# Two row pairs of a 2x2 block product taken by halves in turn, and y kept in empty thirds of its blocks until it is stored

## The chip, the core and the metric

The kernel runs on one core of a Trainium2 chip. The core has TensorE (PE; its weight loads are listed apart as PEld), VectorE (DVE), ScalarE (ACT), GpSimd (POOL) and SyncE (SP), each with its own instruction queue, and 16 DMA engines that all queues share. The metric is device microseconds of one execution. Before the change it is 2008.89 us, the median of three runs (2005.96 to 2012.94).

## The reference

First a long causal convolution along the sequence, written with FFTs; then a mixing layer whose large part is two products with 5696 x 5696 matrices:

```python
batch, seq, d_model = (8, 5696, 128)
# convolution: x (8, 5696, 128), h (5696, 128)
Yf = np.fft.rfft(x, n=2*S, axis=1) * np.fft.rfft(h, n=2*S, axis=0)[None]
x = np.fft.irfft(Yf, n=2*S, axis=1)[:, :S, :]
# mixing
theta = x @ w_theta
zr, zi = x * np.cos(theta), x * np.sin(theta)
y = np.einsum('ts,bsd->btd', w_tok_r, zr) + np.einsum('ts,bsd->btd', w_tok_i, zi)
u = x + y
out = u + np.maximum(u @ w_ch, 0.0)
```

Inputs and output are float32.

## The kernel before

**Set-up and convolution.** Tables of sines and cosines are made first: `r_index` and `r_table` for `r_u`, `r_v`, and `e_index` and `e_table` for `e_t`, in nine steps `E_STEPS` of four columns. For a table GpSimd writes an index and rounds it, VectorE subtracts (`below_one`, L164) and takes the absolute value (`absolute`, L167), and ScalarE takes the sines. While the set-up is written, `tc.manual_schedule` keeps VectorE, ScalarE and GpSimd in the order of the code; a second such block, for VectorE and ScalarE, begins after `load_x(1)`, with `below_one(*r_at[n])` as its first lines. An instruction that stands in no such block, or in another one, is placed by the framework's scheduler. Then eight groups of the convolution follow, each with stages A (`a`), spectrum (`f`), products (`p`, `q`, L400), C (`c`) and D (`d`), in the order of the strings `PLAN_X`, `PLAN_0` and `PLAN`; `t` in `PLAN_0` is a step of `e_table`. The convolved x, called y in the code, goes to `yt_hbm`, channels first.

**Phase steps.** For each of the 22 tiles of 128 tokens of the first half of the sequence, and for each half `hh` of the batch, `phase_step` transposes y into PSUM (`tpz`, L759), computes theta on TensorE (L545 to L551), copies y to SBUF (`copy`, L764), stores it in `y2_hbm` (L765; the profile writes `y_hbm`), takes sine and cosine on ScalarE (L556 to L558), and multiplies on VectorE (L569, L570) to zr and zi. The SBUF place of y is one of six in turn, in the tail of block 0 (`ring["all"]`). The steps of the first batch half (`steps0`) run beside the last convolution group; those of the second (`steps1`) run inside the first row pair, one after every second product, in the order `order1`.

**Blocks.** z is cut into 11 blocks of 128 contraction rows (`b`, `j` = 0 to 10) for the first half of the sequence (pass `p` = 0), and 11 for the second (`p` = 1). A block tile has seven parts of 1024 elements: the first four are the raw zr and zi of both batch halves, the other three take sums of these (`sum_ops`, L852), which only the seven-product scheme reads; two more sums are made in place over raw parts. The second batch half of blocks 0 to 8 is written straight into the block (`home_of`, L583, queues of SP and POOL), and their first half is loaded from `zr_hbm` by `load_b_half` (L741, POOL's queue). Blocks 9 and 10 go through `zr_hbm` whole and are loaded after the last step by `load_b` (L727, ACT's queue).

**Row pairs.** Weight rows `tt` and `22 + tt` make a pair; with `w_tok_r` and `w_tok_i` as columns that is a 2x2 block product. Pairs 0 and 1 of pass 0 use the plain eight products (`plain`, L1247), all others a seven-product scheme (L1326), with sums of weights made by VectorE. Contraction runs in stretches of three blocks (`TJ`), two stretches to a chunk of weights, the second of the second chunk with two blocks. Weights come in by GpSimd's queue (`load_w`, L650, four DMAs for each of a chunk's four operands) into a ring of six places; VectorE transposes them (`w_t`, L919), one stretch ahead (`prepare`), into five and four buffers. `chunks` sets the order: all stretches of pair 0, then all of pair 1, and so on. The loop over `stretches` writes the program; `i` is the stretch's number. At `i == 1` the first two stretches of pair 0 are multiplied with the 22 steps between the products, then come `i == 2` (by batch halves) and the rest. VectorE follows the order of the code up to block 6 of pair 2.

**Around it.** `sum_some` puts owed block sums between products. At a pair's end its PSUM banks are added to y (`addend` loads it from `y2_hbm` or `yt_hbm`) and the result goes to `cp_hbm` (`finish`). `aside` writes a background step (`spread`: phases of the second half of the sequence, `bg_phase`, and small weight transposes, `bg_left`) into stretches that do not end a pair.

Of the kernel before, what the change touches and what calls it, by code (L numbers as in the profile page):

```python
# [10 lines left out]
F32 = mybir.dt.float32  # L11
# [12 lines left out]
def kernel(  # L24
# [683 lines left out]

    place_of, home_of = {}, {}

# [35 lines left out]
    def phase_step(ti, hh, store=nc.sync, odd_eng=None):  # L746

        st = sides["phases"]
        yT = st["end"][ti] if hh == 0 and ti in st["end"] else st[hh][:, :, ti * P:(ti + 1) * P]
        if hh:  # L750
            tags_ = ((f"m{M2}", f"m{M6}"), (f"m{M4}", "misc"))[len(steps1) % 2]
            theta_ps = mps.tile([P, 512], F32, tag=tags_[0], name="theta_ps")
            tpz = mps.tile([P, 4, P], BF16, tag=tags_[1], name="tpz")
        else:
            ps = psum()
            theta_ps = ps[:, 0, :]
            tpz = ps[:, 1, :].bitcast(BF16)[:, :512].rearrange("p (b t) -> p b t", b=4)
        for b in range(4):
            nc.tensor.transpose(tpz[:, b, :], yT[:, b, :], ident_bf)  # L759
        k = st["n"] = (st.get("n", 0) + 1) % 6  # L760
        y_ap = ring["all"][:, WB + 4096 + 512 * k:WB + 4608 + 512 * k].rearrange("p (b d) -> p b d", b=4)

        def copy():
            nc.vector.tensor_copy(y_ap, tpz)  # L764
            store.dma_start(y2_hbm[ti].rearrange("p b d -> p (b d)")[:, 512 * hh:512 * hh + 512],  # L765
                          y_ap.rearrange("p b d -> p (b d)"))
# [89 lines left out]

    done = {"used": 0}
    owed = []

    def sum_some(n):  # L860
# [278 lines left out]

    nxt, second, st = None, None, {}  # L1140
    ordered = ExitStack()
    for i, (k, p, tt, j0, s0, nj) in enumerate(stretches):
        if (p, tt, j0 + s0) in ((0, 0, 0), (1, 0, 0)):
            ordered.enter_context(tc.manual_schedule(engines={mybir.EngineType.DVE}))
        elif (p, tt, j0 + s0) in ((0, 2, 6), (1, 1, 0)):
            ordered.close()
        first_of_pair = j0 + s0 == 0
        end_of_pair = j0 + s0 + nj == NJ
        if first_of_pair and tt == pairs[p][0]:
            if p == 1:  # L1150
                start_pass(p)
            else:
                nxt = prepare(0)
                ms = [mps.tile([P, 512], F32, tag=f"m{q}", name=f"m{q}") for q in (M3, M5, M1, M7)]
                pool_order.enter_context(tc.manual_schedule(engines={mybir.EngineType.Pool}))
# [76 lines left out]
        if first_of_pair and i:  # L1232
            ms = [mps.tile([P, 512], F32, tag=f"m{q}", name=f"m{q}") for q in (range(7) if not classic else (M3, M4, M5, M2) if p else (M2, M6, M1, M7))]
        if first_of_pair:
            where = ((tt, 1), (22 + tt, 0), (tt, 0), (22 + tt, 1))
            if zl is not None:
# [7 lines left out]
        def product(a, jj, j, n, hs):  # L1244
            for r in range(2):
                for h in hs:
                    nc.tensor.matmul(ms[n // 2 * 2 + h], a[n][:, j, :, r],  # L1247
                                     bts_of[p][jj][n % 2 * 2 + h][:, r, :],
                                     start=(n % 2 == 0 and jj == 0 and r == 0), stop=False)

        if i == 0:
            continue
        if i == 1:
            for q, (h, s) in enumerate(((0, 0), (0, 1), (1, 0), (1, 1))):
# [13 lines left out]
        if i == 2:  # L1268
            for h in range(2):
                for n in range(4):  # L1270
                    for j in range(nj):
                        product(a, j0 + s0 + j, j, n, (h,))
                        if j != 1 and h + n:
                            sum_some(1)
            continue
        if classic:
            for n in range(4):
                for j in range(nj):
                    product(a, j0 + s0 + j, j, n, range(2))
# [27 lines left out]
        else:  # L1307
# [4 lines left out]
            if end_of_pair:  # L1312
# [4 lines left out]
                        M1: ((c11, c11, add), (c22, c22, add)),  # L1317
                        M7: ((c11, c11, add),), M6: ((c22, c22, add),)}
            while owed and owed[0][0] < j0 + s0 + nj:
                sum_some(1)  # L1320
            for n, q in enumerate(ORDER):
# [67 lines left out]
```

## Time and profile before

| | us |
|---|---|
| median of three runs | 2008.89 |
| the profiled execution's own time | 2009.51 |
| its span in the trace | 2007.7 |
| convolution with the first batch half's steps | 0 to 363 |
| second batch half's steps, in pair 0 | 363 to 418 |
| rest of pair 0 | 418 to 447 |
| pair 1 | 447 to 486 |
| pairs from 2 on, both passes | 486 to 2007.7 |

All times in the views are microseconds from the span's start, unless marked ns. In a timeline row stand start, duration, engine, line, operation, output<-inputs, shapes and count; the bracket at the end is the engine's idle time before it and what ended that. A row of waits has who waited and for what, then total, times and longest. A window row has, for each engine, busy time and number of instructions, then TensorE's granted clock as a share of full speed, the share of the DMA engines' time that was busy, and what they moved. A row of DMA issues has the queue (SPq, ACTq, POOLq), the count, the size of one and the median time from issue to landing. Buffer numbers are left out of names.

### The profile page before, as it was taken

Reading aid. Unit: us, or ns where it says so; the run is one execution under the profiler, and the core shown is the slowest. Engines: PE = TensorE matmul, PEld = TensorE weight load, DVE = VectorE, ACT = ScalarE, POOL = GpSimd, SP = SyncE. Lnnn points to the kernel's source line nnn. Section 1 sums busy time; section 2 is a strip of 40 time slices with the busy share of each in tenths; the row PEclk is TensorE's granted clock in tenths of the full one; section 3 lists DMA queues with packets and bytes.
Section 4 is the critical chain, followed back from the end, with each engine's and each line's share of the span. In section 5 each row is a group of like instructions: output and inputs, shape, how many; then the busy total and the mean of one; then the engine's idle time right before and its main releaser. Section 6 shows DMA issues by size and latency. Waiting matters only on the chain.

```text
span 2007.7 us, 41091 instructions
## 1 busy us (share of the span) xinstructions
PE 1920.4 (96%) x15581; PEld 1064.4 (53%) x15757; DVE 1557.9 (78%) x2897; ACT 646.5 (32%) x965; POOL 963.0 (48%) x1727
## 2 busy tenths in 40 slices
PE   5898998789999999999999999999999999999998
PEld 5798997544444444444444444444444444444444
DVE  7977887776888888888876779677686776867767
ACT  5998997832323233332300001011111111111112
POOL 7633223463445454453656555545545455354550
PEclk8999999989999999999999999999999999999999
DMA  9989779997899999898999799878869778787893
GB/s 123 60 96 144 91 111 231 279 226 137 151 180 176 181 162 170 173 184 167 178 169 146 136 267 215 134 135 143 151 123 157 135 138 151 130 148 142 141 156 82
DMA packets 489238, 312.02 MB, mean 155 GB/s; under 512 B 184471, under 2 KB 450199, under 8 KB 488055
## 3 DMA queue, kind: packets, MB, share of 16 engines
q0 software_dynamic: 321504, 154.90, 61.6%
q1 hardware_dynamic: 160368, 140.73, 23.9%
q10 hardware_dynamic: 7168, 13.76, 1.9%
q8 instruction: 123, 2.02, 0.4%
q14 instruction: 75, 0.61, 0.1%
HBM read 354.37 MB, written 90.29 MB: 221 GB/s over the span
## 4 chain that ended last, share of the span: by engine, by line
PE 66%; DVE 4%; DMA 3%; issue 2%; ACT 0%; POOL 0%; DVEq 0%
PE m L1326 61%; DVE c L1333 2%; DMA b<-z_hbm 1%; PE utp L999 1%; PE v L1006 1%; PE m L1330 1%; DVE wt L919 1%; PE m L1214 1%; PE theta_ps L534 0%; PE tpz L947 0%; DMA c<-cp_hbm 0%; DMA cp_hbm<-c 0%; DMA z_hbm<-mag 0%; DVE b L852 0%; PE m L1247 0%
## 5 line engine op out<-in xcount | busy, mean ns | idle before, releaser
L650 POOL DMA_DIRECT2D ring<-in_moe_w_tok_i_dram x720 | 388.3, 547 | 652.4 <-DVE wt L919 559.5
L919 DVE STREAM_TRANSPOSE wt<-ring 128x384 f32<-128x384 f32 (+2 forms) x720 | 359.1, 523 | 121.9 <-PE m L1326 57.2
L650 POOL DMA_DIRECT2D ring<-in_moe_w_tok_r_dram x720 | 387.1, 549 | 122.7 <-DVE wt L919 68.8
L1326 PE MATMUL m<-b,wt 128*128 128x512 bf16 x1605 | 384.8, 379 | 4.1 <-DVE wt L919 2.1
L1326 PEld LDWEIGHTS <-wt 128*128 128x128 bf16 x1804 | 176.0, 98 | 216.5 <-DVE wt L919 5.1
L1333 DVE TENSOR_TENSOR c<-c,m 128x512 f32<-128x512 f32 x412 | 265.2, 668 | 0.4 <-PE m L1326 0.4
L1001 ACT ACTIVATE ring<-utp 128x512 bf16<-128x512 bf16 x85 | 50.7, 597 | 575.2 <-PE utp L999 575.2
L139 POOL DMA_DIRECT2D x<-in_x_dram x128 | 99.1, 790 | 119.0 <-PE ps L255 110.5
L421 PE MATMUL ps<-r_u,uv 128*128 128x128 f16 x1024 | 125.6, 222 | 11.0 <-DVE uv L400 6.4
L421 PEld LDWEIGHTS <-uv 128*128 128x128 f16 x2048 | 120.8, 99 | 13.0 <-DVE uv L400 6.7
L421 PE MATMUL ps<-r_v,uv 128*128 128x128 f16 x1024 | 125.2, 221 | 0.0
L1247 PE MATMUL m<-b,wt 128*128 128x512 bf16 x471 | 112.7, 387 | 12.8 <-DMA b<-zr_hbm 9.1
L400 DVE TENSOR_TENSOR uv<-xs,hs 128x1024 f16<-128x1024 f16 x192 | 117.7, 661 | 7.5 <-ACT xs L396 5.9
L996 ACT ACTIVATE ub<-c 128x512 bf16<-128x512 f32 x88 | 55.1, 629 | 185.8 <-DMA ring<-wl_hbm 103.8
L396 ACT ACTIVATE xs<-ps 128x1024 f16<-128x1024 f32 x96 | 88.2, 994 | 4.5 <-PE ps L278 1.6
L1247 PEld LDWEIGHTS <-wt 128*128 128x128 bf16 x528 | 51.5, 99 | 70.5 <-issue 14.9
L949 ACT ACTIVATE ring<-tpz 128x512 bf16<-128x512 bf16 (+1 forms) x46 | 27.4, 597 | 145.9 <-PE tpz L947 127.2
L536 ACT ACTIVATE red<-theta_ps,magic 128x512 f32<-128x512 f32 (+1 forms) x46 | 31.6, 687 | 129.9 <-PE theta_ps L534 101.3
L1008 DVE SCALAR_TENSOR_TENSOR c<-v,c 128x512 f32<-128x512 f32 x88 | 59.8, 682 | 2.6 <-PE v L1006 2.6
L852 DVE TENSOR_TENSOR b<-b 128x1024 bf16<-128x1024 bf16 x100 | 61.3, 680 | 0.0
L278 PEld LDWEIGHTS <-w_t 64*128 64x128 f16 x3240 | 54.2, 97 | 12.1 <-issue 5.9
L556 ACT ACTIVATE mag<-red 128x512 f32<-128x512 f32 (+1 forms) x46 | 29.0, 631 | 92.9 <-DVE red L538 92.9
(2927 smaller groups left out, 3643.2 us busy)
## 6 DMA issues: line engine op xcount, KB each, us to landing
ring<-in_moe_w_tok_r_dram POOLq DMA_DIRECT2D x352, 96.0 KB, 4.6
ring<-in_moe_w_tok_i_dram POOLq DMA_DIRECT2D x352, 96.0 KB, 4.9
ring<-in_moe_w_tok_r_dram POOLq DMA_DIRECT2D x352, 80.0 KB, 4.5
ring<-in_moe_w_tok_i_dram POOLq DMA_DIRECT2D x352, 80.0 KB, 4.0
cp_hbm<-c SPq DMA_DIRECT2D x88, 256.0 KB, 2.3
c<-cp_hbm SPq DMA_DIRECT2D x88, 256.0 KB, 4.4
out_dram<-c SPq DMA_DIRECT2D x88, 256.0 KB, 4.3
yy<-y_hbm SPq DMA_DIRECT2D x84, 128.0 KB, 2.4
```

The costliest lines, as they stand in the source:

```text
L139: nc.gpsimd.dma_start(x16[p0:p1, e, n0:n0 + 16, :HD], bass.AP(tensor=src.tensor, offset=src.offset + (p0 * N2 + n0) * D + dh * HD, ap=[[N2 ...
L396: nc.scalar.activation(xs[:, :, :, :CHK[c][1]], ps, AF.Copy)
L400: nc.vector.tensor_tensor(uv[e][:, :, :, c0:c0 + ck], xs_of[c][:, e:e + 1, :, :ck].to_broadcast([P, 2, HD, ck]), h_part(c), op=mult)
L421: nc.tensor.matmul(o, uv_t[e][:, r, d * K1:d * K1 + P], r_, start=(r == 0), stop=(r == 1))
L650: nc.gpsimd.dma_start(wb[32 * i:32 * i + 32, :ng, :nj * 64], bass.AP(tensor=a.tensor, offset=a.offset + row0 * S + p * H + i * QR + j0 * 6 ...
L852: return [lambda f=f, x=x: f(*x) for f, x in ((nc.vector.tensor_sub, (bt[M3], b12, b22)), (nc.vector.tensor_sub, (bt[M4], b21, b11)), (nc. ...
L919: nc.vector.transpose(wt.rearrange("p j t r -> p (j t r)").bitcast(F32).rearrange("p (j g t) -> p g j t", j=TJ, g=4)[:, :ng, :nj], wb[:, : ...
L996: nc.scalar.activation(ub[:m].rearrange("p b d -> p (b d)"), c[:m], AF.Copy)
L1008: nc.vector.scalar_tensor_tensor(c[:m], v[:m], 0.0, c[:m], op0=ALU.max, op1=ALU.add)
L1247: nc.tensor.matmul(ms[n // 2 * 2 + h], a[n][:, j, :, r], bts_of[p][jj][n % 2 * 2 + h][:, r, :], start=(n % 2 == 0 and jj == 0 and r == 0), ...
L1326: nc.tensor.matmul(ms[q], a[q][:, j, :, r], bts[jj][q][:, r, :], start=(jj == 0 and r == 0), stop=(jj == NJ - 1 and r == 1 and q not in left))
L1333: nc.vector.tensor_tensor(c, z, ms[q], op=op)
```

## The change

It has three parts. In the set-up, `below_one` of both r tables, and the VectorE part of steps 1 and 2 of the e table (`e_turns`), move to the end of the first ordered block, ahead of `load_x(1)`. The first two row pairs are multiplied by halves in turn: blocks 0 to 5 of pair 0, blocks 0 to 5 of pair 1, then 6 to 10 of pair 0, and 6 to 10 of pair 1; so both pairs hold four PSUM banks at once, and no background step runs in pair 1. The y's of the last seven steps of `steps0` and of all of `steps1` are kept in the empty thirds of blocks 4, 3, 7, 8 and 6 (`y_tails`, 512 elements each). Except for tiles 0 and 1 their stores are put off to stretches 2 to 5, where each is written behind a named matmul on SP's queue (`y_some`), and SP now follows the order of the code from pair 0 to block 6 of pair 2. Sums of a block wait until its y's are stored and 28 matmuls have been written since. The first halves of blocks 3 and 4 are loaded inside `steps1` in place of before it.

```diff
-    def e_table(n, n0, cn):
+    def e_turns(n, n0, cn):
         t, k = e_pair(n, cn)
         below_one(t, k)
         absolute(k, t)
+
+    def e_sines(n, n0, cn):
+        t, k = e_pair(n, cn)
         t3, k3 = (z.rearrange("p (n m) -> p n m", m=NB) for z in (t, k))
         sine(e_t[:N1, n0:n0 + cn, 1, :], t3, -1)
         cosine(e_t[:N1, n0:n0 + cn, 0, :], k3)
+
+    def e_table(n, n0, cn):
+        if n not in (1, 2):
+            e_turns(n, n0, cn)
+        e_sines(n, n0, cn)
...
+    for n in range(2):
+        below_one(*r_at[n])
+    for e_ in E_STEPS[1:3]:
+        e_turns(*e_)
     load_x(1)
     e_index(*E_STEPS[4])
     in_order.close()
     in_order.enter_context(tc.manual_schedule(engines={mybir.EngineType.DVE, mybir.EngineType.Activation}))
-    for n in range(2):
-        below_one(*r_at[n])
...
-    chunks = [(p, tt, c) for p in range(2) for tt in pairs[p] for c in range(len(CHUNKS))]
+    chunks = [(0, tt, c) for c in range(len(CHUNKS)) for tt in pairs[0][:2]]
+    chunks += [(p, tt, c) for p in range(2) for tt in pairs[p][2 - 2 * p:] for c in range(len(CHUNKS))]
...
-        k = st["n"] = (st.get("n", 0) + 1) % 6
-        y_ap = ring["all"][:, WB + 4096 + 512 * k:WB + 4608 + 512 * k].rearrange("p (b d) -> p b d", b=4)
+        if y_tails:
+            j, at = y_tails.pop(0)
+            y_flat = place_tail[j][:, at:at + 512]
+        else:
+            j, k = None, (st.get("n", 0) + 1) % 6
+            st["n"] = k
+            y_flat = ring["all"][:, WB + 4096 + 512 * k:WB + 4608 + 512 * k]
...
             nc.vector.tensor_copy(y_ap, tpz)
-            store.dma_start(y2_hbm[ti].rearrange("p b d -> p (b d)")[:, 512 * hh:512 * hh + 512],
-                          y_ap.rearrange("p b d -> p (b d)"))
+            if j is None or ti < 2:
+                y_store()
+            else:
+                y_late.append((j, lambda: y_store(nc.sync)))
...
+    def y_some(n, behind=None):
+        for _ in range(min(n, len(y_late))):
+            j, store = y_late.pop(0)
+            ins = store()
+            y_at[j] = done["n"]
+            if behind is not None:
+                tc.add_manual_dep(ins.ins, behind.ins.name, mybir.DependencyInfo(
+                    mybir.DependencyClass.Sync, mybir.DependencyReason.DATA), reason="y store")
...
-        for o in [o for o in owed if o[1] <= 2 or done["used"] > o[0]][:n]:
+        for o in ([o for o in owed if o[1] <= 2 or done["used"] > o[0]] if forced else
+                  [o for o in owed if (o[1] <= 2 or done["used"] > o[0]) and o[0] < done["ready"] and done["n"] - y_at.get(o[0], -99) > 28
+                   and all(j != o[0] for j, _ in y_late)])[:n]:
             owed.remove(o)
+            while any(j == o[0] for j, _ in y_late):
+                y_some(1)
             o[2]()
+
+    def new_tails(j):
+        place_tail[j] = place_of[j] if j in place_of else home_of[j]
+        y_tails.extend((j, 4096 + 512 * q) for q in range(6))
...
-    for j in range(1, 5):
+    for j in (4, 3):
+        new_tails(j)
+    for j in range(1, 3):
         load_b_half(j)
...
+    for j in (7, 8):
+        place_of[j] = new_b(j, home_pool(j))
+        new_tails(j)
+    new_tails(6)
...
-            if len(steps1) in (17, 18):
+            if len(steps1) in (17, 18, 19, 20):
                 load_b_half(23 - len(steps1))
...
-            ordered.enter_context(tc.manual_schedule(engines={mybir.EngineType.DVE}))
+            ordered.enter_context(tc.manual_schedule(
+                engines={mybir.EngineType.DVE} if p else {mybir.EngineType.DVE, mybir.EngineType.SP}))
...
-            if first_of and spread and (p == 1 or (tt > 0 and (tt, j0 + s0) != (1, 0) and not end_of_pair)):
+            if first_of and spread and (p == 1 or (tt > 1 and not end_of_pair)):
...
-            ms = [mps.tile([P, 512], F32, tag=f"m{q}", name=f"m{q}") for q in (range(7) if not classic else (M3, M4, M5, M2) if p else (M2, M6, M1, M7))]
+            tags_ = ([f"m{q}" for q in (range(7) if not classic else (M3, M4, M5, M2))] if p or not classic
+                     else [f"m{M4}", f"m{M2}", f"m{M6}", "misc"])
+            ms_of[tt] = [mps.tile([P, 512], F32, tag=t_, name=t_) for t_ in tags_]
+        ms = ms_of[tt]
...
                     for j in range(nj):
-                        product(a, j0 + s0 + j, j, n, (h,))
+                        last = product(a, j0 + s0 + j, j, n, (h,))
                         if j != 1 and h + n:
                             sum_some(1)
+                        if j == 1:
+                            y_some(1, last)
+            done["used"] = j0 + s0 + nj
...
                 for j in range(nj):
-                    product(a, j0 + s0 + j, j, n, range(2))
+                    last = product(a, j0 + s0 + j, j, n, range(2))
                     if p == 0 and (n * nj + j) % 4 != 3:
                         sum_some(1)
+                    if p == 0 and (n * nj + j) % 3:
+                        y_some(1, last)
...
-            if p == 0:
-                done["used"] = tt * (j0 + s0 + nj)
+            if p == 0 and tt:
+                done["used"] = j0 + s0 + nj
...
             while owed and owed[0][0] < j0 + s0 + nj:
-                sum_some(1)
+                sum_some(1, True)
```

More of the change, by code (lines that the diff above doesn't have):

```diff
@@ L707 @@
     bts_of = {0: [], 1: []}
-    place_of, home_of = {}, {}
+    place_of, home_of, place_tail = {}, {}, {}
+    y_tails, y_late = [], []
     def new_b(j, pool):
@@ L1138, in in_place @@
             op()
-    nxt, second, st = None, None, {}
+    nxt, second, st, ms_of = None, None, {}, {}
     ordered = ExitStack()
@@ L1153 @@
                 nxt = prepare(0)
-                ms = [mps.tile([P, 512], F32, tag=f"m{q}", name=f"m{q}") for q in (M3, M5, M1, M7)]
+                ms_of[0] = [mps.tile([P, 512], F32, tag=f"m{q}", name=f"m{q}") for q in (M3, M5, M1, M7)]
                 pool_order.enter_context(tc.manual_schedule(engines={mybir.EngineType.Pool}))
@@ L1232 @@
         if first_of_pair and i:
-            ms = [mps.tile([P, 512], F32, tag=f"m{q}", name=f"m{q}") for q in (range(7) if not classic else (M3, M4, M5, M2) if p else (M2, M6, M1, M7))]
+            tags_ = ([f"m{q}" for q in (range(7) if not classic else (M3, M4, M5, M2))] if p or not classic
+                     else [f"m{M4}", f"m{M2}", f"m{M6}", "misc"])
+            ms_of[tt] = [mps.tile([P, 512], F32, tag=t_, name=t_) for t_ in tags_]
+        ms = ms_of[tt]
+        where = ((tt, 1), (22 + tt, 0), (tt, 0), (22 + tt, 1))
         if first_of_pair:
-            where = ((tt, 1), (22 + tt, 0), (tt, 0), (22 + tt, 1))
             if zl is not None:
@@ L1246, in product @@
                 for h in hs:
-                    nc.tensor.matmul(ms[n // 2 * 2 + h], a[n][:, j, :, r],
+                    ins = nc.tensor.matmul(ms[n // 2 * 2 + h], a[n][:, j, :, r],
                                      bts_of[p][jj][n % 2 * 2 + h][:, r, :],
                                      start=(n % 2 == 0 and jj == 0 and r == 0), stop=False)
+            done["n"] += 2 * len(hs)
+            return ins
         if i == 0:
             continue
+        done["ready"] = max(done["ready"], 2 * TJ if tt else j0 + s0 + nj)
         if i == 1:
@@ L1318 @@
                         M7: ((c11, c11, add),), M6: ((c22, c22, add),)}
+            assert not y_late
             while owed and owed[0][0] < j0 + s0 + nj:
-                sum_some(1)
+                sum_some(1, True)
             for n, q in enumerate(ORDER):
```

8 lines of the change are left out of this document (6 added, 2 removed).

## The prediction

> **What bounds the kernel now.** I read the page first, then TensorE's waits, then single stretches. Its lines for the span, the engines and the slices in time:
>
> ```profile
> span 2007.7 us, 41091 instructions
> ...
> PE 1920.4 (96%) x15581; PEld 1064.4 (53%) x15757; DVE 1557.9 (78%) x2897; ACT 646.5 (32%) x965; POOL 963.0 (48%) x1727
> ...
> PE   5898998789999999999999999999999999999998
> ...
> PEclk8999999989999999999999999999999999999999
> ```
>
> TensorE is busy from slice 9 (450 us) to the end. Nothing in the change takes a matmul away, so all there is to win lies ahead of that: the set-up, the 22 phase steps with batches 4 to 7 that run inside the first row pair, and what follows them. Windows by stage (columns: busy of PE, PEld, DVE, ACT, POOL, then granted clock, DMA share, GB/s):
>
> ```profile
> 363.00:418.00 55.00, 47.38 (x394) 29.77 (x401) 43.91 (x83) 41.55 (x71) 32.06 (x60) 0.95 0.98 288
> 418.00:428.50 10.50, 10.45 (x49) 4.79 (x49) 7.44 (x15) 0.00 (x0) 6.33 (x13) 1.00 1.03 204
> 428.50:447.20 18.70, 11.40 (x41) 4.37 (x40) 9.89 (x19) 1.08 (x2) 10.23 (x20) 0.73 1.06 207
> 447.20:486.00 38.80, 38.59 (x195) 18.27 (x196) 27.28 (x48) 9.64 (x16) 12.06 (x23) 1.00 0.68 125
> ```
>
> The third row is the last stretch of the first pair (blocks 9, 10): 11.40 us busy of 18.70 at clock 0.73. The DMA engines are full up to 447 us and have room after it (0.68).
>
> **Part 1, the set-up.** TensorE's and then VectorE's waits between 30 and 62 us (total, times, longest), and from the timeline the operations that are moved:
>
> ```profile
> PE ps L255 <- DVE h L333: 1.9, 2, 1.6
> PE ps L255 <- DVE a__753 L260: 0.6, 1, 0.6
> ...
> DVE uv L400 <- ACT xs L396: 2.6, 1, 2.6
> DVE r_1t L164 <- POOL r_1k L161: 1.8, 1, 1.8
> DVE r_0t L164 <- POOL r_0k L161: 1.1, 1, 1.1
> ```
>
> ```profile
> 37.09 0.29 DVE L164 SCALAR_TENSOR_TENSOR r_0t<-r_0k,r_0t 128x128 f32<-128x128 f32 x1 [1.14 <-POOL r_0k L161]
> ...
> 62.06 0.52 DVE L164 SCALAR_TENSOR_TENSOR e_all<-e_all 89x356 f32<-89x356 f32 x1
> ...
> 62.62 0.34 DVE L167 TENSOR_SCALAR e_all<-e_all 89x356 int32<-89x356 int32 x1
> ```
>
> Although `below_one(r_at)` stands behind the first stage A in the code, VectorE ran both ahead of its evacuations and stood 1.1 + 1.8 us for GpSimd; TensorE waited behind it 1.6 us (of the 1.9) and 0.6 us. After the change both stand inside the written order behind stage A, where GpSimd's tables are long done. They go, with `e_turns` of steps 1 and 2, 2 x 0.29 + 2 x (0.52 + 0.34) = 2.3 us, into the 2.6 us in which VectorE waits for the first `xs`, so that cover just holds; if it doesn't, up to 2.3 us come back, since VectorE's products follow there without a gap. The two `e_turns` taken out at 62 us win nothing: VectorE next waits for matmuls. Gain 1.6 + 0.6 = 2.2 at least if the order takes hold, at most the 2.9 us of waits plus 0.6 us of their own time, 3.5; none if it doesn't. I take **2.5 us**.
>
> **Part 2, the 22 steps.** TensorE's waits between 363 and 415 us, then timeline and issue rows (KB each, us to landing):
>
> ```profile
> PE tpz L759 <- DVE ring L764: 2.8, 2, 1.6
> PE m L1247 <- DMA b<-zr_hbm: 2.0, 1, 2.0
> PE m L1247 <- DMA b<-zz: 1.3, 1, 1.3
> PE m L1247 <- DMA zr_hbm<-zz: 1.1, 1, 1.1
> ```
>
> ```profile
> 370.09 0.42 DVE L764 COPY ring<-tpz 128x512 bf16<-128x512 bf16 x1 [1.90 <-DMA y_hbm<-ring]
> ...
> 379.81 0.57 POOL L741 DMA_DIRECT2D b<-zr_hbm  x1
> ```
>
> ```profile
> y_hbm<-ring SPq DMA_DIRECT2D x16, 128.0 KB, 4.2
> b<-zr_hbm POOLq DMA_DIRECT2D x4, 512.0 KB, 6.8
> ...
> y_hbm<-ring POOLq DMA_DIRECT2D x10, 128.0 KB, 4.4
> ```
>
> Six y places in turn make a copy wait until an old store has landed: 1.9 us of VectorE, 1.6 us of TensorE. With a place of its own for each of the 29 late y's (30 thirds) that wait is gone: **1.6 us**. The other 1.2 us of the first row end on a copy queued behind four transposes, and stay. The 2.0 us is block 5's half: issued at 379.81, landed 6.8 us later, wanted at 385. Its load gets no earlier by the edit, while those of blocks 3 and 4 now stand ahead of it on the same queue: 1 MB more in this stage, against 24 stores of 128 KB (16 + 10 in the rows less the two that stay, 3 MB) less, ten of them gone from GpSimd's queue too. I set that pair at zero. Bounds: all four waits but the 1.2 gone, 6.0 gained; or block 5 later by one whole landing, 6.8 lost.
>
> **Part 3, the late blocks.** Timeline of TensorE, ScalarE's queue, a chain row for the pace, and a window:
>
> ```profile
> 414.57 6.64 PE L1247 MATMUL m<-b,wt 128*128 128x512 bf16 x30
> 419.62 13.04 ACTq L727 DMA_DIRECT2D b<-zr_hbm  x4
> 431.71 0.59 PE L1247 MATMUL m<-b,wt 128*128 128x512 bf16 x2 [2.09 <-DMA b<-zr_hbm]
> 434.52 2.29 PE L1247 MATMUL m<-b,wt 128*128 128x512 bf16 x5 [2.21 <-DMA b<-zr_hbm]
> 439.59 1.86 PE L1247 MATMUL m<-b,wt 128*128 128x512 bf16 x4 [2.77 <-DMA b<-zr_hbm]
> 446.98 0.61 PE L1294 MATMUL m<-ident_bf,yy 128*128 128x128 bf16 x8
> ```
>
> ```profile
> 1356.69 3.24 PE m L1326 x15
> ```
>
> ```profile
> 435.00:440.00 5.00, 2.23 (x7) 0.63 (x6) 2.86 (x5) 0.00 (x0) 2.17 (x4) 0.50 1.24 255
> ```
>
> A full-rate matmul is 3.24/15 = 0.216 us. From 414.57 on the code has 16 matmuls left of the steps, 48 (blocks 6 to 8) and 32 (9, 10), and the identity ones at about 0.9: 96 x 0.216 + 0.9 = 21.6 us. It took until 447.2, 32.6: **11.0 us lost**, 7.1 in the three waits, the rest at the clock of 0.50. Call the end of the steps T (418.0). Now four stretches of 10.4, 10.4, 10.4 and 6.9 us follow: the second pair's blocks 0 to 5, which are all there, then 6 to 8 from T + 20.8, and 9, 10 only from T + 31.2. Their loads, issued from T + 1.6 on, had landed by 439.6, T + 21.6: 9.6 us to spare. So the wait goes. A page of the Trainium skill ("TensorE: Matmul & The Clock Gate", its closing table) asks only that no idle gap pass about 3 us if the clock is to stay up; the longest here is 2.8 and the clock fell all the same, so the measurement decides, and by the rule the loss would be 7.1 and the sum 9.7.
>
> What is late next? Timeline of VectorE (first and last transposes for the stretch that starts at T + 20.8), of weight loads (sixteen from the first row to the second), and of SyncE (a y store in the steps is the last row):
>
> ```profile
> 431.09 1.03 DVE L919 STREAM_TRANSPOSE wt<-ring 128x384 f32<-128x384 f32 x2
> ...
> 437.14 0.58 DVE L919 STREAM_TRANSPOSE wt<-ring 128x384 f32<-128x384 f32 x1 [2.43 <-DMA ring<-in_moe_w_tok_i_dram]
> ```
>
> ```profile
> 420.73 1.11 POOL L650 DMA_DIRECT2D ring<-in_moe_w_tok_r_dram  x2
> ...
> 437.30 0.55 POOL L650 DMA_DIRECT2D ring<-in_moe_w_tok_i_dram  x1 [0.30 <-DMA ring<-in_moe_w_tok_i_dram]
> ...
> 424.67 8.28 SPq L942 DMA_DIRECT2D yT<-yt_hbm  x3
> ```
>
> ```profile
> 404.24 0.74 SPq L765 DMA_DIRECT2D y_hbm<-ring  x1
> ```
>
> The first two operands are there at T + 14, the last at T + 19.7 and wanted at T + 28.6. Weights came at 17.1/16 = 1.07 us a load beside two other busy queues, 17 us for a chunk of sixteen; the stretches want a chunk every 17 to 19. That holds, narrowly. The sums leave the same four owed at the third row pair as before (I walked both loops). Weak is SyncE's queue: three yT loads held it 8.28 us to 433, T + 15; behind them now stand the y stores, and behind their landing VectorE's sums into those thirds, and behind these, in VectorE's fixed order, the transposes for T + 31.2. Ten stores must have landed by about T + 29. At 0.74 us to issue each and 4.2 to land, as in the steps, that is T + 15 + 7.4 + 4.2 = T + 26.6. The c stores and addend loads of both pairs wait in the same queue, but each store's named product is over before theirs, so they come no later than their own results. Two background phases leave the second pair; the 20 later pairs have 60 places for 58 such steps, so they cost nothing. For so small a margin I take off 1.5 us: **9.5 us**, bounds in the rivals and 11.
>
> **Sum.** 2.5 + 1.6 + 9.5 = 13.6. The profiled execution took 2009.51 (span 2007.7 and 1.8 around it), 0.6 over the median of 2008.89: 2009.5 - 13.6 = 1995.9, on the median 1995.3. I forecast **1995.5 us**.
>
> **Rivals.**
> *A, all of it works out:* 3.5 + 6.0 + 11.0 = 20.5, 1989. For it: stores leave a stage with DMA share 0.98. Against: block 5's load is not hurried.
> *B, the half loads get later:* blocks 3 to 5 in a row on one queue cost one landing: 2.5 + 1.6 - 6.8 + 9.5 = 6.8, 2002.
> *C, the stores come out slowly:* with three queues sharing 255 GB/s a store gets 85 GB/s, 128 KB in 1.5 us; ten from T + 15 end at T + 30, landed at T + 34, 5 us late: 2.5 + 1.6 + 11 - 5 = 10.1, 1999 to 2001, as far as later stores add to it. The Trainium skill ("DMA: Bandwidth & Descriptors", "Queues, rings and completion order") says that each DMA engine takes its queues in turn by packets, which is this sharing; the weights' 1.07 us beside two other queues fits it.
> *D, slower than before:* the same place, at the yT loads' 8.28/3 = 2.76 us per store: ten end at T + 42.6, landed at T + 46.8, 17.8 us late, net 15.1 - 17.8 = 2.7 lost, 2012; it makes the kernel slower from about 2.5 us per store. Against: yT rows are 256-byte pieces, and y stores, of 1 KB pieces, issued in 0.74 us in a full stage.
> *E, it doesn't do what it says:* the freed wait is met again in the weights (the 2.43 above), half the 11 comes back: 2001.
>
> **Chances.** Forecast 0.50 (1991 to 2000), A 0.12, B 0.12, C 0.10, E 0.08, D 0.08. Range 1987.5 to 2005 leaves out D and a little of A and B. 0.3% is 6 us, about what this kernel's runs can tell: faster (under 2002.9) is the forecast, A, and most of B, C, E: 0.81; the same 0.11; slower 0.08.
>
> **What would show it.** Right: no VectorE wait on r_0k or r_1k; no wait of L764 on y_hbm; no TensorE wait on b<-zr_hbm past the steps; clock 1.00 there; third pair starting 9 to 11 us earlier from T than 68. Wrong: VectorE's sums (L852) waiting for a y store with TensorE behind them (C, D), a longer wait on b<-zr_hbm inside the steps (B), TensorE waiting on L919 at 6 to 8 (E).

## The result and the profile after

The kernel after took 1998.12 us (median of six runs, 1991.55 to 2004.24), the one before, run beside it, 2010.91 (six runs, 2005.96 to 2015.37): a ratio of 0.9934, 95% interval 0.9906 to 0.9962. The forecast was 1995.5, the range 1987.5 to 2005. Repeated later, the kernel after took 1991.49 (six runs, 1991.05 to 1993.28) beside 2010.02, 0.9901 (0.9877 to 0.9924).

The page of the kernel after, which is of the slowest of its first six runs (2004.24):

```profile
span 2002.4 us, 41243 instructions
...
PE   5898998899999999999999999999999999999998
...
PEclk9899899999999999999999999999999999999999
```

To see where the time went I cut the span at four instructions: the first matmul of stage C (end of the set-up), the first transpose of the second batch half (end of the convolution), the last theta matmul of the 22 steps, and the first matmul of row pair 2. The times are differences of their starts (of the end, for the theta matmul), in us:

| kernel | set-up | convolution | 22 steps | late blocks | from pair 2 on | span |
|---|---|---|---|---|---|---|
| before | 62.21 | 300.86 | 51.67 | 72.45 | 1520.5 | 2007.7 |
| after, first profile | 59.76 | 313.23 | 47.09 | 61.61 | 1520.7 | 2002.4 |
| after, repeated | 58.85 | 300.17 | 46.64 | 61.66 | 1522.1 | 1989.5 |

The three stages that the change touches give 2.45 + 4.58 + 10.84 = 17.9 us in the first profile, and 3.36 + 5.03 + 10.79 = 19.2 in the second. The first one lost 12.4 of it in the convolution, where the edited lines do nothing; the second lost nothing there, and 1.6 from pair 2 on. The two profiles differ by 12.9 us, and almost all of it is the convolution, the same program at a mean granted clock of 0.95 and of 0.98 (third column from the end; the columns are those of the windows in the prediction). First the kernel after, then its repeat:

```profile
59.76:372.99 313.23, 286.47 (x6349) 268.91 (x6349) 241.50 (x352) 275.90 (x358) 109.57 (x158) 0.95 0.85 123
...
235.00:251.00 16.00, 16.00 (x254) 15.43 (x252) 9.29 (x15) 11.22 (x14) 0.00 (x0) 0.57 0.38 85
```

```profile
58.85:359.02 300.17, 275.79 (x6337) 259.36 (x6349) 240.99 (x352) 274.81 (x358) 108.69 (x158) 0.98 0.90 128
```

The second row of the first fence is one of the slow places: TensorE is busy for all 16 us, at a mean clock of 0.57. Such places lie at 127 and 236 us in that one profile.

The windows that answer to those of the prediction, kernel after: the 22 steps in the first row, and in four rows what lies from there to pair 2:

```profile
372.99:420.08 47.09, 43.27 (x386) 27.77 (x386) 38.89 (x73) 39.23 (x67) 25.52 (x48) 0.97 0.97 249
420.08:430.60 10.52, 10.03 (x47) 4.42 (x46) 8.49 (x17) 1.97 (x4) 8.62 (x16) 1.00 0.91 156
430.60:440.90 10.30, 10.30 (x50) 4.64 (x49) 7.21 (x14) 0.00 (x0) 4.25 (x8) 1.00 1.16 262
440.90:451.30 10.40, 10.40 (x50) 4.74 (x49) 6.18 (x12) 0.00 (x0) 0.10 (x1) 1.00 1.04 278
451.30:481.69 30.39, 30.39 (x154) 14.21 (x153) 25.97 (x49) 3.26 (x6) 17.22 (x32) 1.00 1.10 225
```

Before, one stretch of 18.7 us had TensorE busy for 11.4 at a clock of 0.73. Now TensorE is busy throughout after the steps but for half a us, at 1.00. TensorE's only wait there, all between 420 and 486 us (total, times, longest):

```profile
PE m L1299 <- DVE wt L967: 0.5, 1, 0.5
```

The waits on `b<-zr_hbm` past the steps, 7.1 us before, are gone. The loads of blocks 9 and 10 are no earlier for it. ScalarE's queue in the timeline of the kernel after:

```profile
426.87 12.64 ACTq L739 DMA_DIRECT2D b<-zr_hbm  x4
```

Counted as in the prediction, the steps' last 16 products end at T = 420.1 + 16 x 0.216 = 423.5. The loads are issued from T + 3.4 on (T + 1.6 before). TensorE asks for them only at T + 31.2.

The set-up, VectorE's timeline of the kernel after:

```profile
44.47 0.28 DVE L164 SCALAR_TENSOR_TENSOR r_0t<-r_0k,r_0t 128x128 f32<-128x128 f32 x1
44.67 0.28 DVE L164 SCALAR_TENSOR_TENSOR r_1t<-r_1k,r_1t 128x128 f32<-128x128 f32 x1
...
46.24 0.82 DVE L167 TENSOR_SCALAR e_all<-e_all 89x356 int32<-89x356 int32 x1
46.98 7.90 DVE L408 TENSOR_TENSOR uv<-xs,hs 128x1024 f16<-128x1024 f16 x13
```

The moved instructions stand behind stage A without a wait in front of them, and VectorE's products start at once behind them. But TensorE's waits between 30 and 62 us now begin with this row:

```profile
PE ps L278 <- issue: 5.4, 2, 4.1
```

The same place in TensorE's timeline of before:

```profile
55.36 1.83 PE L278 MATMUL ps<-a__753,w_t 64*128 64x64 f16 x107 [1.79 <-issue]
```

"issue" means that TensorE waited for nothing the profile shows. The first spectrum matmul comes 3.3 us earlier than before (44.87 for 48.19); with the longer gap the first of stage C comes 2.45 earlier.

### The profile page after: what moved, and what is told of

Read it like the earlier page. It is cut to its first block, busy times and chain, and to the rows that moved or that the text cites. A ratio compares the mean times of both kernels' runs of the same rounds, so it can differ in the third digit from the quotient of the medians.

```text
span 2002.4 us, 41243 instructions
## 1 busy us (share of the span) xinstructions
PE 1931.3 (96%) x15757; PEld 1069.0 (53%) x15757; DVE 1559.2 (78%) x2897; ACT 647.2 (32%) x965; POOL 957.2 (48%) x1716
## 3 DMA queue, kind: packets, MB, share of 16 engines
q0 software_dynamic: 320976, 153.46, 61.5%
q1 hardware_dynamic: 161952, 142.17, 24.3%
## 4 chain that ended last, share of the span: by engine, by line
PE 72%; DMA 3%; DVE 2%; issue 1%; POOL 1%; ACT 0%; ACTq 0%; DVEq 0%; POOLq 0%
PE m L1387 64%; PE m L1299 3%; DMA b<-z_hbm 2%; PE v L1054 1%; PE utp L1047 1%; DVE c L1394 1%; PE m L1391 1%; PE m L1263 1%; POOL ring L661 1%; PE theta_ps L544 1%; PE tpz L995 1%; PE misc L1299 0%; DVE wt L967 0%; DMA c<-cp_hbm 0%; DMA ring<-in_moe_w_tok_i_dram 0%
```

## The experiments

All of them are edits of the kernel after, unless the text says otherwise. "Steps" and "blocks" are the fourth and fifth columns of the table above. Single executions of one kernel lie up to 14 us apart, so the stages, and not the whole times, carry the readings.

**The order by halves undone.**

```diff
-    chunks = [(0, tt, c) for c in range(len(CHUNKS)) for tt in pairs[0][:2]]
-    chunks += [(p, tt, c) for p in range(2) for tt in pairs[p][2 - 2 * p:] for c in range(len(CHUNKS))]
+    chunks = [(p, tt, c) for p in range(2) for tt in pairs[p] for c in range(len(CHUNKS))]
...
-            done["used"] = j0 + s0 + nj
```

> The changed kernel with pair 0 and pair 1 one after the other again; y in the thirds and its late stores stay. Stage 'blocks' (from the last matmul of step 22 to the first of pair 2; 72.5 us before, 61.6 changed). Theory: the order by halves alone takes the wait for blocks 9 and 10 away: 72 us here, with TensorE waiting on b<-zr_hbm for 7 us and a half clock behind it. Rival: it was the stores' going elsewhere that hurried the blocks' loads: 62 to 66. Second rival: late stores now meet the loads of 9 and 10 on the same DMA engines: 75 or more. Stage 'steps' (first transpose of the second batch half to the last matmul of step 22; 51.7 before, 47.1 changed) stays at 47 in all of them.

2008.89 beside 2008.11 before. Steps 46.42, blocks 74.25, 1.8 more than before. TensorE's timeline of this kernel, its three waits behind the steps:

```profile
426.23 0.59 PE L1298 MATMUL m<-b,wt 128*128 128x512 bf16 x2 [2.06 <-DMA b<-zr_hbm]
428.99 1.01 PE L1298 MATMUL m<-b,wt 128*128 128x512 bf16 x2 [2.17 <-DMA b<-zr_hbm]
435.40 3.14 PE L1298 MATMUL m<-b,wt 128*128 128x512 bf16 x7 [5.40 <-DMA b<-zr_hbm]
```

Without the new order the three waits are back, and the last has doubled (2.77 before). What differs from before at this place is, above all, the held-back y stores, which now meet these loads; that they are what lengthens the last wait is the likeliest reading, not tried by itself.

**The order by halves alone**, with the six y places, the stores, the set-up and SyncE's free order of before.

```diff
...
-    for j in (4, 3):
-        new_tails(j)
-    for j in range(1, 3):
+    for j in range(1, 5):
         load_b_half(j)
...
-    for j in (7, 8):
-        place_of[j] = new_b(j, home_pool(j))
-        new_tails(j)
-    new_tails(6)
...
-            if len(steps1) in (17, 18, 19, 20):
+            if len(steps1) in (17, 18):
...
```

> The order by halves alone: y in six places in turn, stored at once, SyncE in the scheduler's order, halves of blocks 3 and 4 loaded early, old set-up. Theory: 'blocks' 61 to 62 us as in the changed kernel, 'steps' 51 to 52 as before, set-up (to the first spectrum matmul) 48.2. Rival (the late stores are needed for the gain in blocks): 'blocks' 66 or more. Rival for the steps (their gain comes from the order by halves, not from the y places): 'steps' 47.

2000.82 beside 2008.11. Blocks 60.95, steps 51.73, set-up 62.22. The order alone brings the whole gain of the late blocks (11.5 us here), and nothing else.

**The old set-up.**

```diff
...
-    for n in range(2):
-        below_one(*r_at[n])
-    for e_ in E_STEPS[1:3]:
-        e_turns(*e_)
     load_x(1)
...
+    for n in range(2):
+        below_one(*r_at[n])
```

> The changed kernel with the old order of the set-up. Theory: first spectrum matmul at 48.2 us in place of 44.9, first stage C matmul at 62.2 in place of 59.8, with VectorE waiting 1.1 and 1.8 us on r_0k and r_1k; 'steps' 47 and 'blocks' 62 as in the changed kernel; from the first stage C matmul to step 1, 300 to 313 us as the half-rate windows fall, with no tie to the set-up. Rival: the half-rate windows in the convolution (27 us of them in the changed kernel's profile, 8 before) come from the new set-up's timing: 301 here.

1995.89 beside 2008.11. Steps 47.22, blocks 61.40: these don't depend on the set-up. The wait of VectorE on `r_1k` is back (1.8 us), that on `r_0k` only with 0.2 us of the 1.1, and stage C starts at 61.52. With the old set-up it starts between 61.52 and 62.22 (four profiles), with the new one between 58.05 and 59.76 in nine of ten, and at 61.50 in one: the part is mostly worth 1.8 to 4.2 us. The convolution took 303.19 here. Over all profiles it takes 300.86 to 309.44 us with the old set-up and 296.64 to 313.23 with the new one, so nothing says that its slow places are the new set-up's doing.

**Late y stored at once, from places of their own.** What is left of part 2 is then the places, with the later loads of blocks 3 and 4.

```diff
-            if j is None or ti < 2:
+            if True:
```

> The changed kernel with every late y stored right after its copy from its third (queues of SyncE and GpSimd in turn, as before). Theory (each y's own place is what counts, the lateness little): 'steps' 47 to 48.5, no VectorE copy waiting on a store. Rival (the lateness counts, since 24 stores come back into a stage whose DMA engines are full): 'steps' 50 or more, TensorE waiting 4 us or more on b<-zr_hbm and b<-zz. 'blocks' 61 to 62 in both.

1997.65 beside 2008.11. Steps 51.01, against 51.67 before and 47.09: my term for part 2 falls. The copy no longer waits for a place, and yet 0.7 us is all that it brings, little more than the 0.45 by which two profiles of the kernel after differ in this stage. TensorE's waits of this kernel between 361.85 and 412.86 us:

```profile
PE tpz L771 <- ACT ph L567: 3.8, 1, 3.8
PE m L1299 <- DMA b<-zz: 2.8, 2, 2.0
PE m L1299 <- DMA b<-zr_hbm: 2.6, 2, 1.3
PE tpz L771 <- DVE b L785: 1.9, 3, 1.4
```

The wait has moved on from the copy to blocks that come late, 5.4 us (4.4 before, 2.3 in the kernel after). So the gain of the steps lies in the stores that leave the stage. Is it their number, or the queue on which they stood? Four more runs ask that.

**Half of the late y's stored at once, on SyncE's queue.**

```diff
-            if j is None or ti < 2:
+            if j is None or ti < 2 or (hh and len(steps1) % 2):
```

> The changed kernel with every second store of the second batch half made at once (9 of 20 come back into the steps, on SyncE's queue). Theory: the steps are as long as their transfers make them, so the length follows the number of stores: 51.0 with all at once, 47.1 with none, about 48.9 here. Rival (it is the queue of GpSimd, which issues half of the stores between its loads of blocks, that matters): 47 here, since GpSimd issues no more than in the changed kernel.

1990.22 beside 2009.96. Steps 47.17, as if all were held back. Not the number, it seemed, but GpSimd's queue.

**All of them at once, all on SyncE's queue.**

```diff
-            if j is None or ti < 2:
-                y_store()
-            else:
-                y_late.append((j, lambda: y_store(nc.sync)))
+            y_store(nc.sync if hh else store)
```

> The changed kernel, but each late y of the 22 steps is stored at once (none is held back), all on SyncE's queue; nothing of them on GpSimd's. In the run that stored them at once on SyncE's and GpSimd's queues in turn the steps took 51.0 us, against 47.1 in the changed kernel and 47.2 with half of them stored at once on SyncE's queue. Theory (GpSimd's queue: eleven stores standing between its home writes and the block halves are what cost 4 us): steps 46.5 to 48, and VectorE's 4.2 us of waits of block sums on y stores are gone because the stores are long over. Rival (number of stores in this stage: with 24 of 128 KB more it is full): steps 50 to 52, with TensorE waiting some 5 us on blocks.

2001.07 beside 2010.02. Steps 58.26, and my theory of GpSimd's queue is wrong: off that queue the stage gets longer, by 7 us. The rival had foreseen only 50 to 52. TensorE's waits of this kernel between 357.44 and 415.70:

```profile
PE m L1296 <- DMA b<-zz: 9.0, 3, 3.6
PE tpz L771 <- ACT ph L567: 3.8, 1, 3.8
PE m L1296 <- DMA b<-zr_hbm: 2.7, 2, 1.9
PE tpz L771 <- DVE b L785: 1.4, 1, 1.4
```

**The kernel before, with the steps' stores on SyncE's queue.**

```diff
-    steps1 = [lambda ti=ti, n=n: phase_step(ti, 1, nc.gpsimd if n % 2 else nc.sync, ...
+    steps1 = [lambda ti=ti, n=n: phase_step(ti, 1, nc.sync, ...
```

> The kernel before, with one thing changed: the y stores of the 22 steps that go to GpSimd's queue go to SyncE's. The six y places in turn stay. Theory (GpSimd's queue): the steps go from 51.7 to 47.5 to 49.5 (the copy's wait for a place may keep 1 to 2 us), blocks stay at 72 to 74. Rival 1 (the six places, as my prediction had it): the steps stay at 51 to 52.5, with the copy's waits on old stores as long (3.7 us of VectorE's) or longer. Rival 2 (number of stores in a full stage): 51 to 52.5 as well, but with the waits on blocks as before (about 3.3 us of TensorE's).

2020.4 beside 2010.02. Steps 54.65, longer again, with the copy's wait on old stores at 8.6 us of VectorE's (3.7 before). Neither the theory nor either rival had more than 52.5. Blocks 70.24.

**The other half at once, on GpSimd's queue.**

```diff
-            if j is None or ti < 2:
+            if j is None or ti < 2 or (hh and len(steps1) % 2 == 0):
```

> The changed kernel with the other half of the late y's of the 22 steps stored at once: those of the odd steps, on GpSimd's queue, some ten of 128 KB, as many as the run with half of them held back stored on SyncE's. The steps took 51.7 us moving 15.1 MB before, 47.1 moving 11.7 MB in the changed kernel and 47.2 moving 12.8 MB with half stored on SyncE's queue. Theory (bytes: up to some 13 MB they lie beside TensorE's 47 us, at 292 GB/s 13.7 MB would, and only what is above that lengthens the stage): 12.9 to 13.1 MB, steps 46.5 to 48. Rival (GpSimd's queue: stores between its home writes and block halves cost whatever the bytes): 49 to 51, with TensorE's waits on blocks at 5 us, as in the run that stored all at once on both queues.

1994.85 beside 2011.49. Steps 47.74: about as many stores cost 0.6 us more on this queue than on the other, not 2 to 4. With that GpSimd's queue alone is out as the cause of the 4 us. What is left is the load on the DMA engines, or on SyncE's queue, where the stores stand between the writes of z. The view of the DMA engines over just the 22 steps gives their packets. Of before; of the one that stores all at once on both queues; of the one with all on SyncE's:

```profile
DMA packets 9468, 15.09 MB, mean 292 GB/s; under 512 B 2032, under 2 KB 5360, under 8 KB 9460
```

```profile
DMA packets 9406, 14.92 MB, mean 292 GB/s; under 512 B 2036, under 2 KB 5364, under 8 KB 9399
```

```profile
DMA packets 10517, 15.12 MB, mean 259 GB/s; under 512 B 2077, under 2 KB 6770, under 8 KB 10510
```

Of before with SyncE's queue; of half on SyncE's; of half on GpSimd's; and of the kernel after:

```profile
DMA packets 10183, 14.77 MB, mean 270 GB/s; under 512 B 2001, under 2 KB 6481, under 8 KB 10175
```

```profile
DMA packets 8051, 12.77 MB, mean 271 GB/s; under 512 B 1783, under 2 KB 4343, under 8 KB 8044
```

```profile
DMA packets 7118, 12.71 MB, mean 266 GB/s; under 512 B 1744, under 2 KB 3152, under 8 KB 7111
```

```profile
DMA packets 6900, 11.73 MB, mean 249 GB/s; under 512 B 1654, under 2 KB 3190, under 8 KB 6893
```

Bytes, which I had written into the last expectation, put the seven in two groups: 11.7 to 12.8 MB, 47 to 48 us; 14.8 to 15.1 MB, 51 to 58 us. Within the second group they say nothing: 14.77 MB took 54.65 us and 15.09 took 51.67. Packets do. Divided by the length of the steps:

| kernel | packets | steps, us | packets per us |
|---|---|---|---|
| before | 9468 | 51.67 | 183 |
| all at once, both queues | 9406 | 51.01 | 184 |
| before, SyncE's queue | 10183 | 54.65 | 186 |
| all at once, SyncE's queue | 10517 | 58.26 | 181 |
| half at once, SyncE's | 8051 | 47.17 | 171 |
| half at once, GpSimd's | 7118 | 47.74 | 149 |
| after | 6900 | 47.09 | 147 |

The four long ones, and the run of the halves alone (9681 packets, 51.73 us, 187), move 181 to 187 packets per us; all others stay below. That orders the runs, but it is no ceiling of the DMA engines. Right behind the steps, from 420 to 480 us, they move 297 packets per us in the kernel after, at 229 GB/s:

```profile
DMA packets 17825, 13.76 MB, mean 229 GB/s; under 512 B 4854, under 2 KB 15948, under 8 KB 17820
```

And in the two longest runs they were less busy than in the kernel after (share 0.97). The windows of their steps, first all on SyncE's queue (0.81 in its last third, with TensorE still waiting for `b<-zz`), then before with SyncE's queue:

```profile
357.44:415.70 58.26, 44.66 (x379) 28.79 (x386) 42.13 (x79) 39.60 (x67) 29.05 (x55) 0.94 0.91 259
```

```profile
371.54:426.19 54.65, 44.21 (x378) 28.65 (x385) 40.12 (x74) 39.49 (x67) 24.97 (x47) 0.94 0.93 270
```

A count on SyncE's queue orders the runs as well. By the rows of DMA issues it had 67, 69, 71 and 77 transfers under way in the first four runs of the table, 0.74 to 0.77 us of the stage for each; 60 in the fifth and 52 in the last two, 0.79 us or more for each. The way to TensorE shows in VectorE's waits. z is made in seven places in turn, and VectorE waits until the z that last lay in a place has been written out. In the longest run:

```profile
DVE zz L579 <- DMA b<-zz: 5.2, 4, 1.7
...
DVE zz L579 <- DMA zr_hbm<-zz: 2.5, 4, 0.9
...
DVE zz L579 <- DMA ring<-zz: 1.6, 1, 1.6
```

That is 9.3 us. In the first three runs of the table such waits, with those of the copy on old stores, come to 5.1, 3.2 and 9.5 us, in the last three to 0.5 at most. Both counts were made after the runs, and no run tells them apart. Shown is that the stores' leaving the stage is worth 3.9 us, and that half of them is enough; what they fill up there, the DMA engines or SyncE's queue, stays open.

**Early halves and later sums.** Two waits that were left, eased: halves of blocks 3 and 4 loaded ahead of the 22 steps, as before the change, and the block sums still owed at pair 2 kept out of its first two stretches.

```diff
-    for j in range(1, 3):
+    for j in range(1, 5):
         load_b_half(j)
...
-            if len(steps1) in (17, 18, 19, 20):
+            if len(steps1) in (17, 18):
...
-                sum_some(1)
+                if p or tt > 2 or j0 + s0 >= 2 * TJ:
+                    sum_some(1)
```

> The changed kernel with two edits in different stages. (a) Halves of blocks 3 and 4 loaded before the steps again. Theory: they stand in front of block 5's half on GpSimd's queue; without them the waits on b<-zr_hbm inside the steps (2.3 us) shrink to 1 or less and 'steps' is 45 to 46 us. Rival (they are no hindrance): 'steps' stays at 47. (b) The four sums still owed at pair 2 are made in its third stretch in place of its first. Theory: the 1.7 us for which TensorE waits on L967 before that third stretch comes from them; it goes, and 'rest' (from the first matmul of pair 2 to the end; 1520.7) loses 1 to 2 us. Rival: the wait moves to the next stretch, 'rest' unchanged.

1993.44 beside 2009.96. TensorE's wait on `b<-zr_hbm` in the steps falls from 2.3 to 1.0 us, the steps from 47.09 to 46.79 only. A wait of 1.7 us on VectorE's transposes early in pair 2 is gone, and from pair 2 on it takes 1520.5 for 1520.7: given back later.

**SyncE's order left free.**

```diff
-                engines={mybir.EngineType.DVE} if p else {mybir.EngineType.DVE, mybir.EngineType.SP}))
+                engines={mybir.EngineType.DVE}))
```

> The changed kernel with SyncE left to the scheduler in pairs 0 and 1 (the stores still wait for their named matmuls). Theory: the order on SyncE is worth nothing by itself, 'steps' 47 and 'blocks' 61 to 62. Rival: without it loads and stores get in each other's way, VectorE waits longer than 4 us on y stores and TensorE shows it, 'blocks' 63 or more.

1985.55 beside 2009.96, the shortest of all. Yet its steps (46.70) and blocks (61.51) are those of the kernel after; the sums wait longer for y stores, 5.6 us for 4.2, at no cost. What was short is the convolution, 296.64, which the edit doesn't reach. Whether that is chance was asked with the last two, timed beside each other in five rounds.

**The kernel after once more**, nothing edited.

> The changed kernel once more, nothing edited. Theory (its stages give 17.9 us, and a convolution that has anything from 3 to 28 us of half clock moves single executions of either kernel by 6 us either way): ratio 0.9915 to 0.995, steps 47.1, blocks 61.6 and set-up to stage C 59.8 within 0.3 us of the first profile, and first matmul of stage C to the first transpose of the steps 297 to 306 instead of 313. Rival (the changed order of the set-up brings the slow convolution of its first profile): 311 to 315 there again.

**All three eased**: early halves, later sums, SyncE's order free.

> The changed kernel with three things eased: halves of blocks 3 and 4 loaded two steps earlier, background sums of the second pair kept out of its first two stretches, SyncE's order free. Theory (each of them is worth nothing or is given back later): steps 46.5 to 47, blocks 61 to 62, rest 1520 to 1521.5, and the ratio to the kernel before within 0.002 of that of the changed kernel run beside it. Rival (the low single times of the runs that eased one of them, 1993.4 and 1985.6, were theirs and not the convolution's chance): 5 us or more below the changed kernel, ratio 0.989 or less.

The kernel after: 1991.49 (1991.05 to 1993.28), ratio 0.9901 (0.9877 to 0.9924), a little below the range expected for it; set-up 58.85 and steps 46.64, both lower than expected; blocks 61.66, and convolution 300.17, as expected. All three eased: 1991.26 (1989.42 to 1996.78), ratio 0.9902 (0.9878 to 0.9926); steps 46.82, blocks 61.77, convolution 304.22. No edit of mine beats the kernel after; the low single time was its convolution's.

## Why the prediction was right, and where its steps were not

The time was forecast to within 3 us of the first median and 4 us of the second, and the largest term for the right reason. The sum was too small by 4 to 6 us (17.9 and 19.2 for 13.6), and the first profile's convolution hid that. The gain between the first two medians, 12.8 us, comes nearer to 13.6 than the stages do: that is partly luck.

**Set-up, 2.5 us: right.** 2.45 and 3.36 in the two profiles. The waits on `r_0k` and `r_1k` went, the cover for the moved steps held: VectorE's wait for the first `xs` shrank from 2.6 to 0.8 us. Not foreseen was that TensorE's "issue" gap in the spectrum would grow from 1.8 to 4.1 and take part of it back.

**The 22 steps, 1.6 us: wrong in cause and size.** The step that failed is "With a place of its own for each of the 29 late y's (30 thirds) that wait is gone", at 1.6 us, together with "I set that pair at zero". The sign I had named came true, no copy waits for a store, but the places are worth some 0.7 us; the wait met the late blocks instead. The 3 MB of stores that leave the stage, which I had set against block 5's later load at zero, are worth the rest: 51.01 - 47.09 = 3.9. The row that hinted at it was quoted, the DMA share of 0.98, and I used it for rival A alone. It doesn't tell a full stage from one with room, though: it is 0.97 in the kernel after too, at 249 GB/s.

**The late blocks, 9.5 us: right in mechanism, 1.3 too small.** 10.84 and 10.79, the 11.0 that was lost, almost to the last. The 1.5 that I took off for VectorE's waits on late stores cost nothing, although the waits came. SyncE's and then VectorE's timeline of the kernel after:

```profile
435.66 25.36 SPq L782 DMA_DIRECT2D y_hbm<-b  x27
```

```profile
448.42 1.38 DVE L875 TENSOR_TENSOR b<-b 128x1024 bf16<-128x1024 bf16 x2 [3.88 <-DMA y_hbm<-b]
450.15 0.69 DVE L875 TENSOR_TENSOR b<-b 128x1024 bf16<-128x1024 bf16 x1 [0.35 <-DMA y_hbm<-b]
450.76 1.42 DVE L967 STREAM_TRANSPOSE wt<-ring 128x256 f32<-128x256 f32 x4
```

The stores start at 435.66, T + 12.2 (T + 15 in the prediction), and take 25.36 / 27 = 0.94 us each, between the 0.74 of the steps and the 1.5 of rival C, far from the 2.76 of rival D. VectorE stands still for 4.2 us on them, until 450.15, T + 26.7; the prediction had T + 26.6, and T + 29 as the last moment. The transposes behind it end at 452.2, T + 28.7, and TensorE, which starts on that stretch at T + 31.2, doesn't wait. C's mechanism is there, its price is zero: the working was right, and what I took off for its small margin wasn't called for. Pair 2 starts 481.7 - 423.5 = 58.2 us from T (69.0 before, by the same count).

**The clock.** I took the slow stretch of before for a loss that the waits bring. Run by run that holds. The windows of the late blocks, of the run with the order undone and then of the kernel after, repeated:

```profile
408.17:482.42 74.25, 63.37 (x290) 28.42 (x294) 46.83 (x85) 5.44 (x10) 30.76 (x58) 0.93 0.93 194
```

```profile
405.66:467.32 61.66, 60.80 (x290) 28.01 (x294) 47.92 (x88) 5.28 (x10) 30.25 (x56) 1.00 1.07 227
```

The same 290 matmuls, with the three waits at a mean clock of 0.93 and without them at 1.00. The rule that I weighed from the Trainium skill ("TensorE: Matmul & The Clock Gate", the closing table: no idle gap over about 3 us) would have put this loss at 7.1. The gain was 10.8, and the clock of before was at 0.50 from 435 to 440 us behind gaps of 2.1 and 2.2 us, with the one of 2.8 among them. With the order undone it was at 0.50 from 428.6 to 430.0 us, ahead of the gap of 5.40. So gaps of little over 2 us close together were enough here.

**The rivals.** A came nearer than the forecast in the stages, its 20.5 against 17.9 and 19.2, and the reason given for it, stores that leave a busy stage, was the right one for the steps. B: block 5's half did not come a landing later; the wait inside the steps is 2.3 us for 2.0. E: TensorE waits once for transposes, 0.5 us. D: the stores take a third of its price each.

**What the sum had no term for** is the convolution, which lies between 296.64 and 313.23 us over all runs of the two kernels and their variants. It moves a single time by as much as the change is worth.

## What to carry to other kernels

When a late operand stalls a stage, give TensorE other work that is ready, in the order of the program: that alone was worth 11 us, and no faster transfer was needed. A DMA share near 1 doesn't say what a stage is short of: take out half of the transfers, and put the same ones on another queue, before naming a limit. Transfers that leave are worth time only down to the point where something else is the bound (here about 47 us), and half of them would have done. Compare two kernels stage by stage before explaining a whole time; here a stage that the change doesn't touch moved by 12 us.

## What the hardware showed that I had not expected

**A store of the same 128 KB takes three times as many packets on one queue as on the other.** In the run with half at once on GpSimd's queue, eleven y stores stand on that queue (q0) that the kernel after makes on SyncE's (q1); the bytes of the whole are the same. The two queues over the whole span, in the kernel after and then in that run (packets, MB, share of the engines):

```profile
q0 software_dynamic: 320976, 153.46, 61.5%
q1 hardware_dynamic: 161952, 142.17, 24.3%
```

```profile
q0 software_dynamic: 321504, 154.90, 62.2%
q1 hardware_dynamic: 160368, 140.73, 24.2%
```

A store takes (161952 - 160368) / 11 = 144 packets on SyncE's queue and (321504 - 320976) / 11 = 48 on GpSimd's.

**Gaps of 1 to 4 us in which TensorE waits for nothing shown, and a slow clock behind some.** TensorE's timeline of the kernel after, and what its DMA queues moved between 231.5 and 234.5 us:

```profile
234.41 1.26 PE L453 MATMUL ps<-e_t,g__5283 89*128 89x89 f16 x26 [1.80 <-issue]
```

```profile
q8 instruction: 1, 0.02, 2.1%
```

A packet of the instruction queue starts in that stretch, and the gap ends behind it. In the 16 us from 235 us on the mean clock is 0.57, in this profile; in the repeat the same gap is 1.25 us long and the clock stays up. That late instructions make the gap, and the gap the slow clock, was seen in several places but not tried by an experiment; it might explain why single times of these kernels lie up to 14 us apart.
